# Weight pieces one step behind their inputs, two banks of their own, and the inverse one step behind the shrinkage

## The chip, the cores and the metric

The kernel runs on one core of one Trainium2 chip. The metric is the device time of one execution in microseconds (us). The kernel before took 2717.28 us in the median of three runs (2714.53 to 2717.35).

## The reference, cut to what matters

```python
def _attn_ref(x, w_r, w_i, b_r, b_i):          # x: 8 x 3008 x 256
    X = np.fft.rfft(x, axis=1)
    Yr = Xr @ w_r - Xi @ w_i + b_r             # Xr, Xi: real and imaginary part of X
    Yi = Xr @ w_i + Xi @ w_r + b_i
    Yr = np.sign(Yr) * np.maximum(np.abs(Yr) - 0.01, 0.0)      # Yi in the same way
    return np.fft.irfft(Yr + 1j * Yi, n=3008, axis=1).astype(np.float32)

def _moe_ref(x, w_in, w_out):                  # x: 24064 x 256, w_in: 256 x 2048
    h = x @ w_in
    return ((h * np.cos(h)) @ w_out).astype(np.float32)
```

The result is `_moe_ref(_attn_ref(x))`. The two weights of the second part come as 64-bit floats.

## The kernel before

A sequence of 3008 = 64 x 47 points is transformed in two stages per batch. Stage A multiplies by the 47-point transform; stage B does the 64-point transform, the products with the weights, the shrinkage and the inverse of the 64 points, and writes to a scratch tensor in DRAM (`scr`). Stage C (L583 to L625) reads the scratch back (tile `bt`), does the last 47-point transform into a bank `pc` and splits the tokens into a high and a low part (`xTh`, `xTl`). The second part, `moe_step` (L657) and `second` (L628), multiplies tokens by `win` into a bank `ph` (L664 to L666), computes h cos(h) by two activations and a multiplication (L671 to L676), and multiplies by `wo` into two banks `po`. While one batch is in the second part, the stages of the next ones are mixed in between; a planner sets the order there.

Ahead of that lies a prologue, written by hand for batch 0 (`stage_b0`, L456 to L575) under `manual_schedule`, where each engine does its instructions in the written order. Its main loop has twelve steps m. A step has

- on TensorE (PE): product p1 (L499), the forward transform pb for step m + 2 (L487), two products p2 (L511), transposes pq for step m + 3 (L474), the inverse pi (L535), and in some steps one chunk `pa` of stage A for batch 1 (L307);
- on VectorE (DVE): two additions k1 (L503, L504), the sum Xf (L492), four operations on z (L519, L522) and the clamp cl of the shrinkage (L526); the subtraction z - cl (L527) is on GpSimd (POOL), in the last step on DVE;
- on ScalarE (ACT): the scaling of k1 (L505) and the copies out of the banks: X (L491), at (L477), bo (L537), ao (L309). SyncE (SP) issues the writes of bo and ao.

Between these stand the weight pieces. There are sixteen, each 128 x 512 values of 64 bits (`raw`) that `split_f64` (L174) turns into a high and a low part: Abs on ACT (L179), a clamp on POOL (L182) or DVE (L189), two word operations on DVE that build the value `wa` in a PSUM bank (L190, L192), on ACT the cast to the high part (L194) and the scaled low words `wl` (L195), two more operations on DVE (L199, L147), two on POOL (L202, L203). Six pieces are mixed into the loop, one in two steps, two follow at its end (the tail, split in the block that begins at L686), and the last eight come in the second part, through a single buffer `raw` each time. `split_f64` is a generator; each `yield` is a place where the written order goes on with something else. In the loop a piece's clamp is written directly behind its Abs, the cast directly behind the word operations.

PSUM has eight banks: three with tag f, three with h, and o0, o1. In the prologue `fps` (L234) hands out all eight in turn, to pieces as to products.

## Time and profile before

| | |
|---|---|
| median of three runs | 2717.28 us |
| profiled execution | 2712.17 us, span of its instructions 2710.4 us |
| PE busy | 2674.2 us, 99% of the span |
| DVE, ACT, POOL busy | 1773.5, 1788.3, 1014.4 us (65%, 66%, 37%) |
| granted TensorE clock over the span | 0.994 |
| chain that ended last | PE 96%, DVE 2%, ACT 1%, DMA 1% |

PE is busy almost always. The page's slices of 67.8 us show 8 and 7 tenths in the first two slices and 9 in all others, and a granted clock of 9 and 8 tenths in the first two. So the stages that matter for a change in the prologue are read by themselves, in windows and timelines of the first 150 us. In a timeline a row gives the start, the duration, the engine, the source line, what is written from what, the shape, how many instructions were merged into the row, and in brackets how long the engine was idle before and who released it. The pitch of PE instructions is read from differences of starts, since the durations of matmuls overlap.

### The profile page before, as it was taken

The numbers are of one execution on the slowest core, as the hardware profiler recorded it, in microseconds if no ns is written. First come the engines' busy times: TensorE is split into PE (matmuls) and PEld (weight loads), VectorE is DVE, ScalarE is ACT, GpSimd is POOL, SyncE is SP. The second block draws the span as 40 slices with busy tenths as digits, with TensorE's granted clock in tenths as the row PEclk, the third lists the DMA queues.
The fourth block names the chain that finished last, engine by engine and source line by source line (L and its number), as shares of the span: only waits on it lengthen the run. The fifth ranks groups of instructions, "written<-read, shape, count | busy, mean of one in ns | idle before, by whom it ended". The sixth has DMA issues, their size and how long they took to land.

```text
span 2710.4 us, 37830 instructions
## 1 busy us (share of the span) xinstructions
PE 2674.2 (99%) x13466; PEld 2276.6 (84%) x13466; DVE 1773.5 (65%) x3023; ACT 1788.3 (66%) x3392; POOL 1014.4 (37%) x875
## 2 busy tenths in 40 slices
PE   8799999999999999999999999999999999999999
PEld 6478888888888888888888888888888888888888
DVE  4676776666657666666666666666666666756665
ACT  3477666766666666666666666666676666666666
POOL 4575342444424443244432444234342333322222
PEclk9899999999999999999999999999999999999999
DMA  6432121222112221122211221112121111010000
GB/s 179 142 102 82 59 71 57 67 72 76 45 55 69 77 69 54 48 67 71 69 51 54 67 74 63 62 43 77 61 74 55 33 47 58 24 45 30 11 16 15
DMA packets 110253, 168.97 MB, mean 62 GB/s; under 512 B 11344, under 2 KB 60080, under 8 KB 110064
## 3 DMA queue, kind: packets, MB, share of 16 engines
q1 hardware_dynamic: 103216, 144.55, 17.1%
q0 software_dynamic: 6640, 21.81, 2.6%
q8 instruction: 106, 1.74, 0.3%
q14 instruction: 83, 0.68, 0.1%
q10 hardware_dynamic: 208, 0.20, 0.0%
HBM read 94.68 MB, written 71.83 MB: 61 GB/s over the span
## 4 chain that ended last, share of the span: by engine, by line
PE 96%; DVE 2%; ACT 1%; DMA 1%; POOL 0%; issue 0%; ACTq 0%; DVEq 0%; POOLq 0%
PE ph L664 13%; PE po L638 13%; PE ph L665 13%; PE po L639 13%; PE ph L666 13%; PE po L642 13%; PE pc L608 4%; PE pb L372 3%; PE p L398 2%; PE p L397 2%; PE p L396 2%; PE pi L436 2%; PE pa L340 1%; PE pa L342 1%; PE pa L341 1%; PE p L496 1%
## 5 line engine op out<-in xcount | busy, mean ns | idle before, releaser
L144 POOL TENSOR_TENSOR gl<-u,gh 128x512 fp32r<-128x512 f32 (+1 forms) x396 | 503.7, 1272 | 1104.8 <-ACT gh L676 933.1
L672 DVE SCALAR_TENSOR_TENSOR u<-ph,u 128x512 f32<-128x512 f32 (+1 forms) x768 | 520.4, 678 | 359.0 <-ACT u L671 353.6
L675 DVE TENSOR_TENSOR u<-ph,u 128x512 f32<-128x512 f32 (+1 forms) x768 | 521.3, 679 | 314.3 <-ACT u L674 299.5
L671 ACT ACTIVATE u<-ph 128x512 int32<-128x512 f32 (+1 forms) x768 | 450.5, 587 | 310.8 <-PE ph L666 303.6
L674 ACT ACTIVATE u<-u 128x512 f32<-128x512 f32 (+1 forms) x768 | 480.2, 625 | 253.2 <-DVE u L672 250.6
L664 PE MATMUL ph<-xTh,win 128*128 128x512 f32 (+1 forms) x1536 | 613.1, 399 | 3.5 <-DVE u L675 2.5
L638 PE MATMUL po<-gh,wout 128*128 128x512 f32 (+1 forms) x1536 | 601.5, 392 | 0.0
L665 PE MATMUL ph<-xTl,win 128*128 128x512 f32 (+1 forms) x1536 | 596.7, 388 | 0.0
L666 PE MATMUL ph<-xTh,win 128*128 128x512 f32 (+1 forms) x1536 | 595.3, 388 | 0.0
L639 PE MATMUL po<-gh,wout 128*128 128x512 f32 (+1 forms) x1536 | 594.6, 387 | 0.0
L676 ACT CAST gh<-u 128x512 fp32r<-128x512 f32 (+1 forms) x768 | 467.1, 608 | 156.4 <-DVE u L675 154.6
L642 PE MATMUL po<-gl,wout 128*128 128x512 f32 (+1 forms) x1536 | 475.7, 388 | 0.0
L666 PEld LDWEIGHTS ph<-xTh,win 128*128 128x128 f32 x1536 | 289.1, 188 | 56.5
L664 PEld LDWEIGHTS ph<-xTh,win 128*128 128x128 f32 x1536 | 290.2, 189 | 51.2 <-DVE u L675 3.3
L147 DVE TENSOR_TENSOR gl<-u,gh 128x512 fp32r<-128x512 f32 (+1 forms) x372 | 286.4, 770 | 68.6 <-ACT gh L676 65.1
L638 PEld LDWEIGHTS po<-gh,wout 128*128 128x128 f32 x1536 | 289.1, 188 | 49.9
L642 PEld LDWEIGHTS po<-gl,wout 128*128 128x128 f32 x1536 | 285.8, 188 | 53.6
L639 PEld LDWEIGHTS po<-gh,wout 128*128 128x128 f32 x1536 | 289.2, 188 | 49.5
L665 PEld LDWEIGHTS ph<-xTl,win 128*128 128x128 f32 x1536 | 290.1, 189 | 45.1
L422 POOL TENSOR_TENSOR z<-z,cl 128x512 f32<-128x512 f32 x84 | 110.6, 1316 | 220.2 <-DVE cl L421 220.2
L144 POOL TENSOR_TENSOR xl<-xt,xh 96x512 fp32r<-96x512 f32 x96 | 123.9, 1293 | 126.1 <-ACT xh L327 119.1
L608 PEld LDWEIGHTS pc<-last,bt 96*128 96x128 f32 x1024 | 152.2, 195 | 18.9 <-issue 4.1
(119 smaller groups left out, 2926.6 us busy)
## 6 DMA issues: line engine op xcount, KB each, us to landing
scr<-bo SPq DMA_DIRECT2D x96, 256.0 KB, 2.0
bt<-scr SPq DMA_DIRECT2D x127, 192.0 KB, 2.6
scr<-ao SPq DMA_DIRECT2D x112, 192.0 KB, 2.1
at<-scr SPq DMA_DIRECT2D x84, 256.0 KB, 2.8
xt<-in_dram SPq DMA_DIRECT2D x108, 192.0 KB, 2.6
out_dram<-ob SPq DMA_DIRECT2D x80, 256.0 KB, 2.5
fb<-in_dram POOLq DMA_DIRECT2D x48, 256.0 KB, 3.0
raw<-in_dram POOLq DMA_DIRECT2D x16, 512.0 KB, 4.1
```

Of the source, the lines that this page charges most:

```text
L144: return nc.gpsimd.tensor_tensor(out=lo, in0=x, in1=hi.bitcast(F32), op=ALU.subtract)
L638: mm(po[e][:, :n], wo[0][:, 0, f, es], gh[:, :n], start=f == first, stop=False)
L639: mm(po[e][:, :n], wo[0][:, 1, f, es], gh[:, :n], start=False, stop=False)
L642: mm(po[e][:, :n], wo[0][:, 0, f, es], gl[:, :n], start=False, stop=f == last_f)
L664: mm(h, win[:, 0, c, fs], th[:, c, :n], start=c == 0, stop=False)
L665: mm(h, win[:, 0, c, fs], tl[:, c, :n], start=False, stop=False)
L666: mm(h, win[:, 1, c, fs], th[:, c, :n], start=False, stop=c == 1)
L671: nc.scalar.activation(k[:, :n], h, AF.Identity, bias=0.25, scale=1.0 / TWO_PI)
L672: nc.vector.scalar_tensor_tensor(out=u[:, :n], in0=h, scalar=1.0 / TWO_PI, in1=k[:, :n], op0=ALU.mult, op1=ALU.subtract)
L674: nc.scalar.activation(u[:, :n], u[:, :n], AF.Sin, bias=HALF_PI, scale=TWO_PI)
L675: nc.vector.tensor_tensor(out=u[:, :n], in0=h, in1=u[:, :n], op=ALU.mult)
L676: nc.scalar.copy(gh[:, :n], u[:, :n])
```

## The change

`split_f64` has two more `yield`s, behind the Abs and behind the word operations, and `stage_b0` has a function `words(k)` that goes on with piece k by one such part. In an even step m = 2k the clamp of piece k comes first and the second pair of DVE operations of piece k - 1 behind k1; in the odd step the POOL multiplications of k - 1 come first, then the word operations of k, its cast behind the forward transform, and at the end of the step the Abs of piece k + 1. The functions `sums`, `mixed` and `shrink` become one, `pair`, in which the inverse is `idft(m - 1)` instead of `idft(m - 2)`. Pieces of the prologue take banks o0 and o1 alone; `fps` hands out f and h in turn. The two tail pieces begin inside `stage_b0`. The first bt loads all go through SP (one went through ACT), and the rest of the first stage C is written by hand too.

```diff
@@ split_f64
-    def split_f64(hi, lo, raw, ge):
+    def split_f64(hi, lo, raw, ge, bank):
...
         nc.scalar.activation(m, v.bitcast(F32), AF.Abs)
+        yield
         if ge:
...
         yield
         ve = nc.vector
-        a = fps("wa")
+        a = ps.tile([128, 512], F32, tag=bank, name="wa", bufs=1 if bank[0] == "o" else 3)
...
+        yield
         nc.scalar.copy(hi, a)
@@ fps
         if "pro" in pool:
-            if not banks:
-                banks.extend(("f", "h", "o0", "f", "h", "o1", "f", "h"))
-            tag = banks.pop(0)
-            return ps.tile([128, 512], F32, tag=tag, name=name, bufs=1 if tag[0] == "o" else 3)
+            banks.append(name)
+            return ps.tile([128, 512], F32, tag="fh"[len(banks) % 2], name=name, bufs=3)
@@ stage_b0
+        w = {}
+
+        def words(k):
+
+            if 0 <= k < EARLY_W + TAIL_W:
+                if k not in w:
+                    w[k] = piece_steps(k, k < EARLY_W, f"o{k % 2}")
+                next(w[k], None)
+
+        def pair(m, k, odd):
+            words(k - odd)
             p = fps("p1")[:, :256]
...
             nc.scalar.activation(k1[1], k1[1], AF.Copy, scale=sig[:, m:m + 1])
-            K1[m] = k1
-
-        def mixed(m):
+            words(k - 1 + odd)
+            fwd(m + 2)
+            if odd:
+                words(k)
             p, xf = fps("p2"), X.pop(m)
...
-            P[m] = p
-
-        def shrink(m):
-            p, k1 = P.pop(m), K1.pop(m)
+            turn(m + 3)
+            if m == NP - 1:
+                next(a1)
+            idft(m - 1)
             z = wk.tile([128, 2, 256], F32, tag=("z", "yh", "yl")[m % 3], name="z", bufs=2)
...
-        w = None
+        words(0)
         for m in range(NP):
-            if m % 2 == 0:
-                load(m // 2 + 2)
-            sums(m)
-            if w is not None:
-                next(w, None)
-            fwd(m + 2)
-            mixed(m)
-            turn(m + 3)
-            idft(m - 2)
-            shrink(m)
+            k, odd = divmod(m, 2)
+            if not odd:
+                load(k + 2)
+            pair(m, k, odd)
+            if odd:
+                words(k + 1)
+                if len(raws) < EARLY_W + TAIL_W:
+                    load_piece()
             if m < 2 or m in (3, 5, 7, 9):
                 next(a1)
-            if w is not None:
-                next(w, None)
-            if m % 2 == 0:
-                w = piece_steps(m // 2, True)
-                next(w)
-                if len(raws) < EARLY_W + TAIL_W:
-                    load_piece()
+        words(EARLY_W + 1)
+        words(EARLY_W - 1)
+        words(EARLY_W - 1)
         next(a1)
-        idft(NP - 2)
         next(a1)
+        for k in range(2):
+            words(EARLY_W + k)
+            words(EARLY_W + k)
         idft(NP - 1)
-        for _ in w:
-            pass
+        next(a1)
+        return w[EARLY_W], w[EARLY_W + 1]
@@ stage_c
-                (nc.scalar if (b, u) == (0, 1) else nc.sync).dma_start(
+                nc.sync.dma_start(
@@ the block that calls them
     with tc.manual_schedule():
-            stage_b0(a1)
+        tail = stage_b0(a1)
         c00 = stage_c(0, 0)
         next(c00)
-            tail = [piece_steps(EARLY_W + k, False) for k in range(TAIL_W)]
-            for _ in range(5):
-                next(a1, None)
-                for g in tail:
-                    next(g, None)
+        for g in tail:
+            next(g)
+            next(a1)
+        for g in tail:
+            next(g)
         for _ in a1:
             pass
+        for g in tail:
+            for _ in g:
+                pass
+        first.close()
-    del pool["pro"]
+        del pool["pro"]
...
```

What the built programs have in their queues is shown for three places. First ACT in the loop, one pair of steps, in the program before. Here k is the scaling of k1, Xf and at the copies of forward transform and transposes, wm, win and wl a piece's Abs, cast and low words:

```order
L179 ACTIVATE wm<-raw 128x512
L505 ACTIVATE k_566<-k_566,sig 128x256
L194 CAST win<-wa 128x512
L195 ACTIVATE wl<-raw 128x512
L491 COPY Xf<-pb 128x512
L477 COPY at_593<-pq 128x512
L537 COPY bo<-pi 128x512
L309 COPY ao<-pa 96x512
```

The same place on ACT in the changed program:

```order
L525 ACTIVATE k_569<-k_569,sig 128x256
L491 COPY Xf<-pb 128x512
L196 CAST win<-wa 128x512
L197 ACTIVATE wl<-raw 128x512
L477 COPY at_596<-pq 128x512
L506 COPY bo<-pi 128x512
L179 ACTIVATE wm<-raw 128x512
```

The X copy has moved ahead of cast and low words, and the Abs from the front of the step to its end, where it belongs to the next piece.

Second POOL in the loop, one pair of steps before (z is the subtraction of the shrinkage, wm the clamp, wq and win the multiplications):

```order
L527 TENSOR_TENSOR z<-z,cl 128x512
L182 TENSOR_SCALAR wm<-wm 128x512
L171 DMA raw<-in_dram 128x2x512
L527 TENSOR_TENSOR z<-z,cl 128x512
L465 DMA fb<-in_dram 128x512
L202 TENSOR_TENSOR wq<-wl,wq 128x512
L203 TENSOR_TENSOR win<-wr,wq 128x512
```

And POOL in the changed program, one pair:

```order
L171 DMA raw<-in_dram 128x2x512
L465 DMA fb<-in_dram 128x512
L183 TENSOR_SCALAR wm<-wm 128x512
L548 TENSOR_TENSOR z<-z,cl 128x512
L204 TENSOR_TENSOR wq<-wl,wq 128x512
L205 TENSOR_TENSOR win<-wr,wq 128x512
L548 TENSOR_TENSOR z<-z,cl 128x512
```

Clamp and multiplications now stand ahead of the z of their step instead of behind it.

Third PE and ACT behind the first ph. On PE before, from the seventh group of ph products (the one that starts at 147.67 us) to the next pc:

```order
L664 MATMUL ph<-xTh,win 128x512
L665 MATMUL ph<-xTl,win 128x512
L666 MATMUL ph<-xTh,win 128x512
L664 MATMUL ph<-xTh,win 128x512
L665 MATMUL ph<-xTl,win 128x512
L666 MATMUL ph<-xTh,win 128x512
L608 MATMUL pc<-last,bt 128x94 x8
```

On PE in the changed program, from the end of the sixth group to the seventh:

```order
L671 MATMUL ph<-xTh,win 128x512
L672 MATMUL ph<-xTl,win 128x512
L673 MATMUL ph<-xTh,win 128x512
L615 MATMUL pc<-last,bt 128x94 x8
L671 MATMUL ph<-xTh,win 128x512
```

The eight pc matmuls stood behind the eighth group and stand ahead of the seventh now. On ACT in the changed program, from the last of the first pc tiles on:

```order
L628 CAST xTh<-pc 128x2x188
L196 CAST win<-wa 128x512
L678 ACTIVATE u<-ph 128x512
L179 ACTIVATE wm<-raw 128x512
L197 ACTIVATE wl<-raw 128x512
L678 ACTIVATE u<-ph 128x512
L681 ACT_TABLE_LOAD
L681 ACTIVATE u<-u 128x512
```

And the same on ACT before, from the cast of the ninth piece on:

```order
L194 CAST win<-wa 128x512
L671 ACTIVATE u<-ph 128x512 x2
L674 ACT_TABLE_LOAD
L674 ACTIVATE u<-u 128x512
L671 ACTIVATE u<-ph 128x512
L674 ACTIVATE u<-u 128x512
L179 ACTIVATE wm<-raw 128x512
L195 ACTIVATE wl<-raw 128x512
```

The Abs and the low words of the tenth piece (wm and wl from raw) stood behind three activations of ph and the table load, and stand behind the first activation now.

## Rows read from the trace of the kernel before

**Rows 1.** Three stages: us; busy PE, PEld, DVE, ACT, POOL (x); PEclk; DMA share; GB/s

```profile
32.46:119.19 86.73, 67.36 (x301) 48.81 (x300) 54.73 (x119) 35.85 (x69) 44.34 (x38) 0.94 0.41 126
...
130.43:147.67 17.24, 13.98 (x51) 11.94 (x51) 8.79 (x19) 9.53 (x21) 7.64 (x7) 0.61 0.44 133
147.67:300.00 152.33, 152.33 (x726) 126.72 (x726) 105.13 (x168) 116.55 (x222) 92.18 (x77) 1.00 0.28 84
```

**Rows 2.** Waits from 36 to 122 us: who for whom, total us, times, longest

```profile
PE pb L487 <- ACT at L477: 11.8, 5, 3.2
```

**Rows 3.** Timeline, one pair of steps: start, us, engine, line [idle before, releaser]

```profile
41.75 0.69 DVE L190 TENSOR_SCALAR wa<-wm 128x512 uint32<-128x512 uint32 x1 [2.51 <-POOL wm L182]
...
45.37 1.16 PE L487 MATMUL pb<-fb,at 128*128 128x128 f32 x8 [2.32 <-ACT at L477]
...
47.60 1.26 POOL L527 TENSOR_TENSOR z<-z,cl 128x512 f32<-128x512 f32 x1 [5.30 <-DVE cl L526]
...
56.25 0.69 DVE L190 TENSOR_SCALAR wa<-wm 128x512 uint32<-128x512 uint32 x1 [2.49 <-POOL wm L182]
```

**Rows 4.** Timeline, from the last inverse to the first pc

```profile
119.19 1.28 PE L535 MATMUL pi<-z,inf 128*128 128x512 f32 x2 [2.89 <-ACT ao L309]
...
123.30 0.86 SPq L592 DMA_DIRECT2D bt<-scr  x2
...
130.43 5.46 PE L608 MATMUL pc<-last,bt 96*128 96x128 f32 x24 [3.29 <-DVE wr L147]
```

**Rows 5.** Timeline, first ph and the stop behind it

```profile
136.94 1.65 PE L664 MATMUL ph<-xTh,win 128*128 128x512 f32 x3 [1.05 <-ACT xTh L621]
...
139.81 0.60 POOL L171 DMA_DIRECT2D raw<-in_dram  x1 [4.73 <-issue]
...
144.35 0.60 ACT L671 ACTIVATE u<-ph 128x512 int32<-128x512 f32 x1 [1.23 <-PE ph L666]
...
144.97 1.28 ACT L674 ACT_TABLE_LOAD   x1
...
147.67 0.50 PE L664 MATMUL ph<-xTh,win 128*128 128x512 f32 x1 [2.21 <-DVE u L675]
```

**Rows 6.** Timeline, PE: the first p1, then one step without an idle moment

```profile
32.46 1.03 PE L496 MATMUL p<-wr,Xf 128*128 128x256 f32 x4
...
50.24 1.03 PE L496 MATMUL p<-wr,Xf 128*128 128x256 f32 x4
...
51.10 1.05 PE L487 MATMUL pb<-fb,at 128*128 128x128 f32 x8
...
51.99 1.03 PE L496 MATMUL p<-wi,Xf 128*128 128x256 f32 x4
...
53.72 0.60 PE L474 MATMUL pq<-ident,a 128*128 128x128 f32 x4
...
54.16 1.02 PE L535 MATMUL pi<-z,inf 128*128 128x512 f32 x2
...
55.02 1.02 PE L307 MATMUL pa<-xt,fa 96*96 96x512 f32 x2
...
55.88 1.03 PE L496 MATMUL p<-wr,Xf 128*128 128x256 f32 x4
```

**Rows 7.** Timeline, DVE: the shrinkage of one step, its first and last instruction

```profile
45.20 0.84 DVE L519 TENSOR_TENSOR z<-p,k 64x256 f32<-64x256 f32 x2
...
47.08 0.43 DVE L526 TENSOR_SCALAR cl<-z 128x512 f32<-128x512 f32 x1
```

**Rows 8.** Timeline in a later stage: POOL and DVE at the same time

```profile
897.21 1.29 POOL L144 TENSOR_TENSOR gl<-u,gh 128x512 fp32r<-128x512 f32 x1 [7.83 <-ACT gh L676]
...
897.48 1.31 DVE L421 TENSOR_SCALAR cl<-z 128x512 f32<-128x512 f32 x1
```

**Rows 9.** DMA issues of the page: KB each, median us to landing

```profile
bt<-scr SPq DMA_DIRECT2D x127, 192.0 KB, 2.6
...
raw<-in_dram POOLq DMA_DIRECT2D x16, 512.0 KB, 4.1
```

More of the change, by code (lines that the diff above doesn't have):

```diff
@@ L218, in load_piece, with piece_steps @@
             raws.append(load_f64(piece(W_ORDER[len(raws)])[2]))
-    def piece_steps(k, ge):
+    def piece_steps(k, ge, bank="f"):
         while len(raws) <= k:
             load_piece()
-        return split_f64(*piece(W_ORDER[k])[:2], raws[k], ge)
+        return split_f64(*piece(W_ORDER[k])[:2], raws[k], ge, bank)
     def moe_w():
@@ L459, in stage_b0 @@
         dst = scr2[0].rearrange("j g r k d -> (j g r) (k d)")
-        at, fb, X, V, P, K1 = {}, {}, {}, {}, {}, {}
+        at, fb, X, V = {}, {}, {}, {}
         def load(n):
@@ L497, in product, with idft @@
                    skip_group_check=True)
-        def sums(m):
+        def idft(m):
+            if m < 0:
+                return
+            p, y = fps("pi"), V.pop(m)
+            for lo, hi, v in ((0, 256, 0), (256, 512, 1)) if m == 0 else ((0, 512, 1),):
+                mm(p[:, lo:hi], inf[0][:, v], y[:, lo:hi], start=lo == 0, stop=hi == 512, skip_group_check=True)
+            bo = stage_out("bo")
+            nc.scalar.copy(bo, p)
+            nc.sync.dma_start(dst[:, 512 * m:512 * m + 512], bo)
+        w = {}
[6 more added lines that the diff above has]
+            words(k - odd)
             p = fps("p1")[:, :256]
@@ L528, in shrink @@
             V[m] = z
-        def idft(m):
-            if m < 0:
-                return
-            p, y = fps("pi"), V.pop(m)
-            for lo, hi, v in ((0, 256, 0), (256, 512, 1)) if m == 0 else ((0, 512, 1),):
-                mm(p[:, lo:hi], inf[0][:, v], y[:, lo:hi], start=lo == 0, stop=hi == 512, skip_group_check=True)
-            bo = stage_out("bo")
-            nc.scalar.copy(bo, p)
-            nc.sync.dma_start(dst[:, 512 * m:512 * m + 512], bo)
         next(a1)
@@ L685, in tile_body @@
     mw = moe_w()
-    with ExitStack() as first:
-        pool["pro"] = first.enter_context(tc.tile_pool(name="pro", bufs=1))
-        idle = wk.tile([128, 512], F32R, tag="cl", name="idle", bufs=1)
-        nc.vector.memset(idle.bitcast(F32), 0.0)
-        def warm(n):
-            p = ps.tile([128, 512], F32, tag="o0", name="pz", bufs=1)
-            for _ in range(n):
-                mm(p, idle[:, :128], idle, start=True, stop=True)
-        warm(WARM)
-        stage_a0()
-        load_fourier_w()
-        inf[0] = pool["pro"].tile([128, 2, 128], F32, name="inf", bufs=1)
-        load_constants()
-        sum_fourier_w()
-        for _ in range(3):
-            load_piece()
-        with tc.issue_after(mark["x0"].ins):
-            load_split_constants()
-        split_fourier_w()
-        a1 = stage_a1()
-        with tc.manual_schedule():
-            stage_b0(a1)
-            c00 = stage_c(0, 0)
-            next(c00)
-            tail = [piece_steps(EARLY_W + k, False) for k in range(TAIL_W)]
-            for _ in range(5):
-                next(a1, None)
-                for g in tail:
-                    next(g, None)
-            for _ in a1:
-                pass
@@ L719, in tile_body, with warm @@
-    del pool["pro"]
-    pool["mo"] = ctx.enter_context(tc.tile_pool(name="mo", bufs=2, reuse_waits="tile"))
-    for _ in c00:
-        pass
+    first = ExitStack()
+    pool["pro"] = first.enter_context(tc.tile_pool(name="pro", bufs=1))
+    idle = wk.tile([128, 512], F32R, tag="cl", name="idle", bufs=1)
+    nc.vector.memset(idle.bitcast(F32), 0.0)
+    def warm(n):
+        p = ps.tile([128, 512], F32, tag="o0", name="pz", bufs=1)
+        for _ in range(n):
+            mm(p, idle[:, :128], idle, start=True, stop=True)
@@ new lines, in tile_body @@
+    warm(WARM)
+    stage_a0()
+    load_fourier_w()
+    inf[0] = pool["pro"].tile([128, 2, 128], F32, name="inf", bufs=1)
+    load_constants()
+    sum_fourier_w()
+    for _ in range(3):
+        load_piece()
+    with tc.issue_after(mark["x0"].ins):
+        load_split_constants()
+    split_fourier_w()
+    a1 = stage_a1()
+    with tc.manual_schedule():
+        tail = stage_b0(a1)
+        c00 = stage_c(0, 0)
+        next(c00)
+        for g in tail:
[3 more added lines that the diff above has]
+            next(g)
+        for _ in a1:
+            pass
+        for g in tail:
+            for _ in g:
+                pass
+        first.close()
+        del pool["pro"]
+        pool["mo"] = ctx.enter_context(tc.tile_pool(name="mo", bufs=2, reuse_waits="tile"))
+        for _ in c00:
+            pass
```

## The prediction

> **What bounds the kernel now.** I read the page first: TensorE is busy for 99% of the span, so only its idle moments and its slow clock can be won back, and the page's slices show them in the first 150 us alone. Then the windows view by stage: from the first p1 product to the last inverse PE is busy for 67.36 of 86.73 us, from the first pc to the stop behind the first ph products for 13.98 of 17.24 us at a mean granted clock of 0.61, and from there to 300 us for all of 152.33 us [rows 1]. So what the change wins in the loop of twelve steps and in the passage to the second part reaches the end of the kernel, because behind 147.67 us TensorE has no gap that could swallow it.
>
> Then the waits view of the loop: the largest wait of PE is pb on the copy of the transpose, ACT at L477, five times, 11.8 us [rows 2]. The timeline says what holds ACT: pairs of steps repeat every 14.50 us (L190 at 41.75 and 56.25 us), and a pair is one chain. DVE sits 2.51 us until POOL has clamped the piece (L182), ACT's cast L194 stands ahead of the X copy and the at copy and waits for DVE's two word operations, and PE's pb comes after that with 2.32 us idle; POOL's subtraction of z has itself waited 5.30 us for DVE [rows 3]. Nobody is full: everybody waits for an operation whose input was started just before.
>
> At the end of the loop 11.24 us pass between the last inverse (119.19) and the first pc (130.43), the last 3.29 of them for a DVE operation of a tail piece whose wa sat in a bank that pc needs, although the first bt load had been issued at 123.30 [rows 4]. From pc to the first ph 6.51 us pass, and from there to the seventh L664 (147.67) another 10.73 us, at whose end PE stands still for 2.21 us until DVE's multiplication frees a bank of ph [rows 5].
>
> **The change part by part.** No arithmetic is added or removed: the same operations of pieces, products and inverses are written in another order, the eight prologue pieces take banks o0 and o1, the rest rotates over six banks instead of eight.
>
> *The loop.* Every operation of a piece is now issued one step after its input, so cast L196 finds its wa done, and the X copy goes ahead of it; the at copy has no piece's chain before it. What remains is PE's own work. One step without an idle moment gives the pitches by differences of starts: p1 0.86, pb 0.89, the two p2 products 1.73, transposes 0.44, inverse 0.86, a chunk of the other batch 0.86 us [rows 6]. Between the first p1 and the last inverse the new order has 12 p1, 12 p2, 10 pb, 9 groups of transposes, 11 inverses and 9 chunks: 10.3 + 20.8 + 8.9 + 4.0 + 9.5 + 7.7 = 61.2 us. DVE is busy for 54.73 us in the old loop and does the same work [rows 1], so it fits beside.
>
> Moving the inverse from two steps behind to one takes slack away. Between the end of p2 and the inverse of the same step PE now has transposes, inverse, p1, pb, p2, transposes: 0.44 + 0.86 + 0.86 + 0.89 + 1.73 + 0.44 = 5.22 us. The shrinkage needs 1.88 us on DVE to the start of cl (45.20 to 47.08), 0.52 from there to POOL's start (47.60) and 1.26 on POOL [rows 3, 7]: 3.66 us. 1.56 us are left per step. Only the last step has less: behind the last p2 stand one inverse and three chunks, 3.44 us, so the last inverse waits at least 0.2 us.
>
> POOL works more during DVE's cl than before, when it always waited for cl. The price of such a meeting stands in a later stage: a cl that starts 0.27 us after a POOL operation takes 1.31 us, and it takes 0.43 in the loop of before [rows 7, 8]. That is 0.9 us each. The Trainium skill, "SBUF — State Buffer", section "Who interferes with whom", states such a lock: DVE and GpSimd share one port pair, and whoever comes second is blocked for the other's whole instruction; the two rows agree, since cl ended 0.29 us after the POOL operation did. By that rule all twelve cl and the last subtraction on DVE could be hit; by the loop's own rows none was.
>
> In the order of POOL the clamp or the two multiplications now end before the z of their step, so I expect one hit, at the last z, where the last multiplications run. I take 0.2 + 0.9 and another 1.4 us for waits in single steps that no row prices: 2.5 us, between 0 (PE never waits) and 12 (the first rival). The last inverse then starts at 32.46 + 61.2 + 2.5 = 96.2 us instead of 119.19: a gain of 23.0 us.
>
> *From the last inverse to pc.* No piece lies in a bank of pc any more, so pc waits for its data alone. Inverse to bt issue took 4.11 us (119.19 to 123.30) [rows 4], and bt lands after 2.6 us in the median [rows 9]: 6.7 us. ACT now has two Abs and two chunk copies ahead of the last bo copy, each with a buffer to wait for, so I take 8.0, between 6.7 and the old 11.24: a gain of 3.2 us.
>
> *From pc to ph* all sixteen pc matmuls come first (twelve before), 6.51 us in the old run; I take 6.0, between 4.5 at full clock and 6.5: 0.5 us.
>
> *The stop behind the first ph.* ACT's order changes for the worse: the Abs of the next piece, which needs the next raw transfer, now stands behind one activation of ph, before the second activation and the table load. That transfer is issued on POOL when the words of the piece before have been read, 2.87 us after the first ph in the old run [rows 5]; the new order does this earlier, I take 1.0 us after. Landing takes 4.1 us [rows 9], three ACT instructions of at most 0.60 us follow, and from table load to the restart of PE 2.70 us passed [rows 5]: 1.0 + 4.1 + 1.8 + 2.7 = 9.6, and I take 10.0 us against 10.73, between 8 and 14: a gain of 0.7. PE stands still longer, but eight pc matmuls that came after the restart now come before it, 8 x 0.22 (a quarter of pb's pitch) = 1.8 us of work inside the stop.
>
> *The clock.* The old run lost 0.39 of 17.24 us, 6.7 us of full-speed work, to the granted clock around the passage [rows 1], partly while waiting anyway. PE goes idle there again, before pc and behind the first ph, so part of the slow stretch may reach past the restart: a loss of 3 us, between 0 and 6.7.
>
> Sum: 23.0 + 3.2 + 0.5 + 0.7 + 1.8 - 3.0 = 26.2 us. The sum was made on the profiled execution, 2712.17 us (span 2710.4 and 1.8 around it), which becomes 2686 us. The median of the runs shown is 2717.28, 5.1 above it; the forecast in those terms is 2717.3 - 26.2 = 2691 us.
>
> **Rivals.**
>
> *Half of the loop's gaps come back.* If cl meets POOL in most steps, DVE has 54.73 + 12 x 0.9 = 65.5 us of work against PE's 61.2, and 0.9 of each step's 1.56 us of slack is gone. With that the loop would last some 9.5 us longer than I take it (4.3 from DVE's load, some 0.45 in each of eleven steps from late z), so 2700 us. For it speaks the 1.31 us cl [rows 8]; against it that POOL's work has a step of lead and ends before cl.
>
> *No change that can be measured.* The remaining eight pieces pass through one raw buffer; if their pace set the second part, an earlier start would only wait for them, and the time would be 2717 less 0 to 5 us, about 2714. Against it: PE was busy for all of the 152.33 us in which they arrived [rows 1].
>
> *Slower.* The Abs waiting for a raw transfer now stands ahead of activations of ph. If not only the first of the seven raw transfers of the second part stops PE but all of them do, each costs what the first costs. Between the first ph and its stop PE had 10.73 - 2.21 = 8.52 us of work at a mean clock of 0.61 [rows 1, 5], 5.2 us at full clock; four pc go out of it (0.9) and eight come in (1.8), 6.1 us, so that 3.9 of the 10.0 us are stop. Seven times that is 27 us; with the gain of the loop alone it makes 2717 - 23 + 27 + 5 (six such stops would also let the clock fall; I put a quarter of 3.9 us on each) = 2726 us. It decides from some 3.4 us per piece on. Against it: in the old run raw transfers came just as late for ACT, and PE did not stop [rows 1]; the later ones have three steps of finished activations in hand.
>
> **How the numbers follow.** Forecast 0.77, half of the loop 0.13, no change 0.06, slower 0.04. The forecast's own range by its bounds is 2684 to 2698 us (clock at nothing and no waits in the loop; or the passage and the stop at their upper ends). The range for 8 in 10 reaches over the first rival: 2685 to 2705. Within 0.2% (5.4 us, about what a measurement here can tell from no change) lies the second rival and a bit of the others: 0.07; faster 0.89; slower 0.04.
>
> **What would show it.** Right: in the new profile PE's gaps before pb are gone, pairs repeat every 10 to 11 us instead of 14.50, the last inverse starts at 95 to 98 us, the first pc waits for a transfer and not for DVE, the first ph comes at 109 to 112 us, and PE stands still behind it for 4 to 5 us until a DVE multiplication that hangs on raw. Wrong: PE waiting at the inverse for POOL's z in most steps, cl of 1 us and more in the loop, a last inverse behind 105 us, or idle PE behind 150 us.

## The result and the profile after

The changed kernel took 2685.09 us in the median of four runs (2682.84 to 2687.74), beside 2717.32 us of the kernel before (four runs, 2714.53 to 2718.47): a ratio of 0.9883, 95% interval 0.9866 to 0.9900. The forecast was 2691 us with a range of 2685 to 2705, so the time lies just inside the range's lower edge. The profiled execution took 2687.74 us, with a span of 2686.0 us against 2710.4.

The windows by stage, as in [rows 1]: loop, passage with the stop, and the time from the restart to 300 us (columns: us; busy PE, PEld, DVE, ACT, POOL; PEclk; DMA share; GB/s):

```profile
34.54:96.72 62.18, 61.33 (x303) 47.11 (x301) 53.74 (x119) 36.55 (x69) 44.41 (x38) 1.00 0.56 177
106.22:122.47 16.25, 12.20 (x67) 11.16 (x67) 8.88 (x19) 8.44 (x19) 4.88 (x5) 0.82 0.61 186
122.47:300.00 177.53, 177.28 (x830) 147.14 (x831) 125.49 (x202) 132.88 (x252) 104.02 (x87) 0.98 0.25 78
```

The loop is 62.18 us long where it was 86.73, and PE is busy in all of it but 0.85 us, with the same work as before on DVE (53.74 us against 54.73). Of the 24.55 us gained, 18.52 are idle time of PE (19.37 us before) and 6.03 are shorter busy time for the same matmuls (67.36 to 61.33 us): the mean granted clock rose from 0.94 [rows 1] to 1.00, so PE ran at 2.4 GHz throughout, where it had run at 1.2 GHz for a part of the time. That the loop began 2.08 us later than in the old trace (34.54 against 32.46) took part of the gain back; the first experiment shows that executions of one program differ by as much.

The wait of 11.8 us of pb for ACT [rows 2] is gone. These are waits of the new loop (who for whom: total us, times, longest):

```profile
POOL z L548 <- DVE cl L547: 14.8, 11, 3.6
...
ACT at L477 <- PE pq L474: 8.4, 5, 1.9
...
ACT win L196 <- DVE wa L193: 2.5, 4, 0.7
...
ACT wout L196 <- DVE wa L193: 1.7, 2, 1.1
```

ACT's at copy now waits for PE and no longer PE for it: the direction of the wait has turned, which is what a stage looks like when PE has become its bound. The cast still waits for DVE, for 0.7 us at most in the four pieces of `win` and for 1.1 at most in the two of `wout`. One pair of steps, as in [rows 3]:

```profile
50.62 1.05 PE L487 MATMUL pb<-fb,at 128*128 128x128 f32 x8
...
51.12 1.28 POOL L548 TENSOR_TENSOR z<-z,cl 128x512 f32<-128x512 f32 x1 [1.31 <-DVE cl L547]
...
51.74 0.68 DVE L191 TENSOR_SCALAR wa<-wm 128x512 uint32<-128x512 uint32 x1
...
53.19 0.58 ACT L196 CAST win<-wa 128x512 fp32r<-128x512 f32 x1 [0.62 <-DVE wa L193]
...
62.17 0.68 DVE L191 TENSOR_SCALAR wa<-wm 128x512 uint32<-128x512 uint32 x1
```

The word operation L191 starts with no wait for the clamp (2.51 us before), pb with no wait for ACT, and a pair repeats after 10.43 us (51.74 to 62.17) instead of 14.50. From the last inverse to the first pc, as in [rows 4]:

```profile
96.72 1.12 PE L504 MATMUL pi<-z,inf 128*128 128x512 f32 x2 [0.86 <-DVE z L548]
...
98.45 0.59 ACT L506 COPY bo<-pi 128x512 f32<-128x512 f32 x1
...
99.07 0.34 SPq L507 DMA_DIRECT2D scr<-bo  x1
...
103.34 1.31 SPq L599 DMA_DIRECT2D bt<-scr  x3
...
106.22 5.21 PE L615 MATMUL pc<-last,bt 96*128 96x128 f32 x24 [4.08 <-DMA bt<-scr]
```

The first pc waits for the transfer alone: ACT copies bo 1.73 us behind the start of the inverse, SP issues the write 0.62 us later, the bt issue comes 4.27 us behind that, and the load takes 2.88. And the stop behind the first ph, as in [rows 5]:

```profile
112.56 0.94 PE L671 MATMUL ph<-xTh,win 128*128 128x512 f32 x3
...
114.08 0.60 POOL L171 DMA_DIRECT2D raw<-in_dram  x1 [6.05 <-ACT xTh L628]
...
116.74 1.92 PE L615 MATMUL pc<-last,bt 96*128 96x94 f32 x16
...
118.05 0.67 ACT L179 ACTIVATE wm<-raw 128x512 f32<-128x512 f32 x1 [2.72 <-DMA raw<-in_dram]
...
119.77 1.28 ACT L681 ACT_TABLE_LOAD   x1
...
122.47 0.80 PE L671 MATMUL ph<-xTh,win 128*128 128x512 f32 x1 [3.81 <-DVE u L682]
```

ACT stands 2.72 us before the Abs of the tenth piece, the table load comes only then, and PE stands still for 3.81 us until DVE's multiplication.

### The profile page after: what moved, and what is told of

It is laid out like the page before. It is cut to its first block, busy times and chain, and to the rows that moved or that the text cites. A ratio compares the mean times of both kernels' runs of the same rounds, so it can differ in the third digit from the quotient of the medians.

```text
span 2686.0 us, 37841 instructions
## 1 busy us (share of the span) xinstructions
PE 2664.3 (99%) x13466; PEld 2272.8 (85%) x13466; DVE 1772.8 (66%) x3023; ACT 1789.5 (67%) x3392; POOL 1014.4 (38%) x875
## 4 chain that ended last, share of the span: by engine, by line
PE 97%; DMA 1%; DVE 1%; ACT 0%; issue 0%; SPq 0%; POOL 0%; ACTq 0%; DVEq 0%
PE ph L671 13%; PE po L645 13%; PE po L646 13%; PE ph L672 13%; PE po L649 13%; PE ph L673 13%; PE pc L615 4%; PE pb L372 3%; PE p L398 2%; PE p L397 2%; PE p L396 2%; PE pi L436 2%; PE p L496 1%; PE pa L340 1%; PE pa L342 1%; PE pa L341 1%
## 5 line engine op out<-in xcount | busy, mean ns | idle before, releaser
L683 ACT CAST gh<-u 128x512 fp32r<-128x512 f32 (+1 forms) x768 | 466.9, 608 | 153.6 <-DVE u L682 151.8
L615 PEld LDWEIGHTS pc<-last,bt 96*128 96x128 f32 x1024 | 151.1, 194 | 19.9 <-ACT wm L179 4.9
```

The source lines that it names most:

```text
L683: nc.scalar.copy(gh[:, :n], u[:, :n])
```

## The experiments

The theory was that the chain between the engines made the old loop long: an operation whose input was started just before holds up its engine's queue, and everything behind it. Rivals were that the banks or the inverse carry the gain, and later ones for the passage and the stop; a letter in an expectation stands for what that expectation says of it. All kernels were profiled, and one table reads them together, in us: first p1; loop (first p1 to last inverse); last inverse to pc; pc to the first ph; from there to the seventh matmul of the line of L664; from that to the 101st; and, as the sum of the five, first p1 to the 101st.

| kernel | median of the runs | first p1 | loop | to pc | to ph | to 7th | to 101st | sum |
|---|---|---|---|---|---|---|---|---|
| before | 2717.32 | 32.46 | 86.74 | 11.24 | 6.51 | 10.72 | 151.0 | 266.2 |
| changed | 2685.09 | 34.54 | 62.18 | 9.50 | 6.33 | 9.91 | 151.8 | 239.7 |
| changed, 2nd profile | 2682.75 | 31.17 | 62.18 | 8.29 | 4.76 | 10.40 | 150.9 | 236.5 |
| changed, 3rd profile | 2683.98 | 30.82 | 62.18 | 7.76 | 5.62 | 10.00 | 150.6 | 236.2 |
| e1 | 2688.18 | 34.92 | 65.10 | 8.91 | 6.07 | 9.75 | 151.5 | 241.4 |
| e2 | 2683.14 | 34.55 | 61.42 | 9.12 | 7.15 | 7.62 | 150.3 | 235.6 |
| e3 | 2711.03 | 31.40 | 86.07 | 8.63 | 10.19 | 9.86 | 151.0 | 265.8 |
| e4 | 2707.19 | 34.16 | 87.05 | 6.70 | 5.07 | 10.62 | 151.1 | 260.6 |
| e5 | 2692.69 | 34.79 | 67.81 | 11.86 | 6.80 | 8.84 | 149.5 | 244.8 |
| e6 | 2680.88 | 31.61 | 61.41 | 9.38 | 7.14 | 7.87 | 150.1 | 235.9 |
| e6, 2nd profile | 2682.78 | 34.72 | 61.41 | 9.46 | 7.15 | 7.55 | 150.2 | 235.8 |
| i1 | 2680.53 | 31.96 | 62.18 | 7.99 | 7.15 | 7.87 | 150.2 | 235.4 |
| i2 | 2684.48 | 34.67 | 62.18 | 8.48 | 5.55 | 9.55 | 150.7 | 236.5 |
| i4 | 2683.77 | 36.32 | 61.15 | 8.13 | 8.74 | 7.27 | 150.4 | 235.7 |

From the 101st matmul to the last one it is 2407.1 us in each of these profiles. So nothing that was done here reaches behind the first 300 us, and one execution differs from another by its sum and its first p1.

**The changed kernel again, twice**, as an anchor beside other kernels.

> The changed kernel itself, as the anchor for the three others of this set. Both theories: 2680 to 2688 us, with the first p1 product at 32 to 35 us, the last inverse 61 to 63 us behind it, and PE idle for 3 to 4 us behind the first ph products.

> The changed kernel once more, beside the kernel of e6 on the same chip. 2680 to 2688 us; loop 62.18 us whatever the opening takes; PE stops 3 us or more behind the first ph products or runs on a slow clock there.

Measured: 2682.75 us (2681.25 to 2684.94; ratio 0.9888, 0.9875 to 0.9902) and 2683.98 us (2680.54 to 2686.52; 0.9894, 0.9877 to 0.9910). The loop is 62.18 us in all three profiles of the program, and the first p1 comes at 34.54, 31.17 and 30.82 us. Two details of the second profile missed what was expected: its first p1 is earlier than 32 us, and PE stood still behind the first ph products for 4.29 us and not 3 to 4. In the third it was 2.48 us, at a granted clock of 0.80 from the first ph to that stop. The later start of the first profile is thus not the change's: the opening alone differs by up to 3.7 us between executions of one program, and the kernels of before (32.46, 31.40) lie within that. What remains of the spans is compared from the first p1 on, by the sum: 266.2 less 239.7, 236.5 and 236.2, a gain of 26.5, 29.7 and 30.0 us.

**e1: the old banks.** The changed kernel with the rotation over eight banks, to pieces as to products.

```diff
-        a = ps.tile([128, 512], F32, tag=bank, name="wa", bufs=1 if bank[0] == "o" else 3)
+        a = fps("wa")
```

> The changed kernel, except that pieces and products rotate through all eight banks as in the kernel before. Theory A (the gain of the loop comes from the order of the pieces' operations, banks matter only where pc waits for a piece): the loop from the first p1 to the last inverse stays at 62 to 65 us, the passage to pc grows by 0 to 3 us, the whole is 0 to 5 us slower than the changed kernel, 2685 to 2690 us. Theory B (the banks carry much of the gain): the loop is 70 us or longer, the whole above 2697 us.

Measured: 2688.18 us (2683.17 to 2689.84; 0.9908, 0.9894 to 0.9923). The loop is 2.92 us longer (65.10, just over the 62 to 65 of theory A and far from theory B's 70); p2 waits twice for a bank that a piece still reads, 2.3 us together. This is one of the two:

```profile
48.42 1.13 PE L498 MATMUL p<-wi,Xf 128*128 128x256 f32 x4 [1.15 <-DVE wr L147]
```

**e2: the old inverse.** The changed kernel with the inverse two steps behind the shrinkage.

```diff
-            idft(m - 1)
+            idft(m - 2)
...
         next(a1)
+        idft(NP - 2)
         next(a1)
```

> The changed kernel, except that the inverse stands two steps behind the shrinkage, as in the kernel before. Theory A: PE never waited for z with 1.6 us of slack, so more slack wins nothing in the loop (61 to 63 us); the last inverse stands behind one more inverse instead of a wait, so the whole is within 3 us of the changed kernel, 2682 to 2688 us. Theory C (the inverse's place carries part of the gain): the loop grows by 5 us or more, the whole is above 2690 us.

Measured: 2683.14 us (2677.98 to 2683.95; 0.9889, 0.9874 to 0.9904). The loop is 0.76 us shorter without this part of the change, since the last inverse no longer waits for z.

**e3: the banks alone**, in the kernel before: pieces of the prologue in o0 and o1, the rest over f and h.

```diff
-            if not banks:
-                banks.extend(("f", "h", "o0", "f", "h", "o1", "f", "h"))
-            tag = banks.pop(0)
-            return ps.tile([128, 512], F32, tag=tag, name=name, bufs=1 if tag[0] == "o" else 3)
+            banks.append(name)
+            return ps.tile([128, 512], F32, tag="fh"[len(banks) % 2], name=name, bufs=3)
```

> The kernel before, with the two banks for pieces alone and six for the rest, the order of operations as before. Theory A: the loop keeps its 86.7 us, the pairs their 14.5 us; pc no longer waits for DVE's wr, which wins 3 us of the passage at most: 2712 to 2719 us. Theory B (banks): the loop shortens by 8 us or more, the whole is below 2708 us.

Measured: 2711.03 us (ten runs, 2708.84 to 2713.90), before 2712.9 (19 runs); ratio 0.9995, 0.9985 to 1.0004: no change, though the median lies 1 us below what was expected. The passage to pc is 2.6 us shorter (8.63 for 11.24), as theory A allowed, but pc to ph is 3.7 us longer, where the second group of pc waits 3.21 us for ACT's copy of a chunk (ao). The loop is 86.07 us and waits as before:

```profile
DVE wa L190 <- POOL wm L182: 15.8, 6, 3.3
...
PE pb L486 <- ACT at L476: 10.3, 5, 3.2
```

**e4: the word operations directly behind the clamp.** The changed kernel, but in the pieces of the loop DVE's two word operations are written directly behind POOL's clamp; the cast stays a step behind them.

```diff
             nc.gpsimd.tensor_scalar(out=c, in0=m, scalar1=F64_TINY, scalar2=F64_HUGE, op0=ALU.max, op1=ALU.min)
-        yield
+        if not ge:
+            yield
...
         yield
+        if ge:
+            yield
         nc.scalar.copy(hi, a)
```

> The changed kernel, except that the two word operations of a piece on DVE are written directly behind POOL's clamp again; cast and low words on ACT keep their later place. Theory A (each operation that stands directly behind its input holds up its whole engine): DVE waits for the clamp (1.92 us, itself behind two DMA issues of POOL) in each pair, k1 and z come later by that and the inverse waits for z: pairs of 12.5 to 14.5 us, loop of 73 to 84 us, the whole 2696 to 2708 us. Theory D (the place of the cast on ACT ahead of the X and at copies was the cause by itself): the loop stays below 66 us, the whole below 2690 us.

Measured: 2707.19 us (ten runs, 2706.04 to 2708.73; 0.9978, 0.9968 to 0.9988). The loop is 87.05 us, longer than expected and as long as in the kernel before, and DVE waits for the clamp in every pair; this is one of the six:

```profile
49.71 1.93 POOL L183 TENSOR_SCALAR wm<-wm 128x512 f32<-128x512 f32 x1
...
51.68 0.69 DVE L192 TENSOR_SCALAR wa<-wm 128x512 uint32<-128x512 uint32 x1 [4.45 <-POOL wm L183]
...
53.52 0.51 ACT L528 ACTIVATE k<-k,sig 128x256 f32<-128x256 f32 x1 [6.00 <-DVE k L526]
...
54.40 0.59 ACT L480 COPY at<-pq 128x512 f32<-128x512 f32 x1
...
55.04 1.62 PE L490 MATMUL pb<-fb,at 128*128 128x128 f32 x8 [2.99 <-ACT at L480]
```

The row to read is DVE's: 4.45 us of waiting for the clamp, with the two k1 additions queued behind, so ACT's scaling waits 6.00 us, X and at copies come behind it, and pb is 2.99 us late. So one operation written directly behind its input is enough to lose as much as the whole change had won in the loop.

It is not the old link put back, though. In the kernel before, the clamp stood at the end of one step and the word operations behind the k1 additions of the next; here both stand at the front of a step, ahead of k1, and the clamp behind two DMA issues of POOL. The waits of DVE for the clamp are half as long again as they were. The first line is of the kernel before, the second of e4 (36 to 122 us):

```profile
DVE wa L190 <- POOL wm L182: 16.3, 6, 3.3
...
DVE wa L192 <- POOL wm L183: 24.8, 6, 4.6
```

Nor does the sum of 24.8 us explain the 24.87 us of the loop one to one, near as the two figures are. Of what PE lost, 17.58 us are idle time and 7.29 are longer busy time, at a mean granted clock of 0.94 instead of 1.00. The windows row of the loop:

```profile
34.16:121.21 87.05, 68.62 (x304) 49.93 (x303) 55.48 (x120) 36.23 (x71) 44.47 (x38) 0.94 0.42 131
```

**e5: the cast behind the word operations again.** The changed kernel, but cast and low words are written directly behind the word operations.

```diff
-        yield
         nc.scalar.copy(hi, a)
         nc.scalar.activation(low, pair[:, :, 0], AF.Copy, scale=2.0 ** -52)
         yield
+        yield
```

> The changed kernel, but the cast and the scaled low words of a piece on ACT are written directly behind the two word operations of DVE, as in the kernel before; the word operations stay one step behind the clamp. Theory A, with POOL to DVE as its first link: the cast waits for two word operations, 1.4 us, with only the copy of the transposes behind it, and PE's slack takes most of it: loop 0 to 4 us longer than the 62 us of the changed kernel, 2683 to 2690 us in all. Rival B (the cast ahead of the copies on ACT is what held PE): waits of pb for ACT come back, 8 us or more in the loop, 2693 us or more.

Measured: 2692.69 us (five runs, 2691.61 to 2693.35; 0.9924, 0.9912 to 0.9937), 9.9 us more than the changed kernel beside it: more than the theory said, less than the rival. My expectation overlooked that in this order the cast stands ahead of the X copy as well, not of the at copy alone:

```profile
54.19 0.59 ACT L195 CAST win<-wa 128x512 fp32r<-128x512 f32 x1 [1.09 <-DVE wa L193]
...
55.84 0.42 DVE L492 TENSOR_TENSOR Xf<-pb,Xf 128x256 f32<-128x256 f32 x1 [1.69 <-ACT Xf L491]
...
58.64 1.27 POOL L548 TENSOR_TENSOR z<-z,cl 128x512 f32<-128x512 f32 x1 [2.65 <-DVE cl L547]
...
59.96 1.13 PE L504 MATMUL pi<-z,inf 128*128 128x512 f32 x2 [0.23 <-POOL z L548]
```

DVE waits 1.69 us for X with the operations on z queued behind, so POOL and then the inverse are late, and not pb as in the rival. The loop loses 5.6 us, 2.0 of them as idle time of PE and 3.6 as longer busy time at a mean granted clock of 0.97. Another 3.6 us go in the passage (11.86 against 8.29): the cast of a tail piece stood ahead of the last bo copy, which came at 109.01 us, 6.40 behind its inverse.

**e6: the order of the pieces alone.** The edits of e1 and e2 together: old banks, old inverse.

> The changed kernel with the bank rotation of before and the inverse two steps behind, as before: what is left of the change is that every operation of a piece is written one step behind its input, and with it the new order of pieces, bt loads and tail. Theory A (this order carries the gain, banks and inverse carry at most a few us): 2682 to 2692 us, a loop of 62 to 66 us. Rival (banks and order are needed together, since wa holds a bank that the loop's products want): a loop over 70 us and over 2695 us.

> The kernel of e6 (order of the pieces alone, banks and inverse as before) beside the changed kernel on the same chip. If banks and inverse carry nothing and ACT's order behind the first ph is worth what i1 showed, 1 to 4 us faster than the changed kernel, 2678 to 2684 us, with a loop of 61.4 us and a stop under 1 us behind the first ph. If the first measurement of e6 was a favourable draw, within 1 us of the changed kernel.

Measured: 2680.88 us (2678.98 to 2682.69; 0.9875, 0.9858 to 0.9891), and in a second set 2682.78 (2680.79 to 2684.02; 0.9885, 0.9871 to 0.9900) beside 2683.98 of the changed kernel. The loop is 61.41 us in both profiles, and PE is busy in all of it but 0.08 us:

```profile
34.72:96.13 61.41, 61.33 (x303) 47.16 (x302) 53.84 (x119) 36.07 (x68) 44.45 (x38) 1.00 0.56 176
```

So the order carries the whole gain of the loop; banks and inverse add nothing to it. The first set came out under the 2682 us that had been expected at the least. The waits for a bank that e1 showed do not come here: they belong to the old rotation with the new inverse. Whether e6 beats the changed kernel by some 1 us the intervals don't tell.

What e6 keeps is still a bundle. In the loop it holds the places of the word operations (e4), of the cast and the X copy (e5), of the Abs, and of POOL's clamp and multiplications, which stand ahead of z now. The last two were not tried alone, nor was any one of these moved by itself in the kernel before.

**i1: the Abs behind the Sin.** The changed kernel; the Abs of a piece of the second part may only come behind the first Sin.

```diff
-        nc.scalar.activation(m, v.bitcast(F32), AF.Abs)
+        with tc.issue_after(mark["sin"].ins) if "sin" in mark else ExitStack():
+            nc.scalar.activation(m, v.bitcast(F32), AF.Abs)
...
-        nc.scalar.activation(u[:, :n], u[:, :n], AF.Sin, bias=HALF_PI, scale=TWO_PI)
+        sin = nc.scalar.activation(u[:, :n], u[:, :n], AF.Sin, bias=HALF_PI, scale=TWO_PI)
+        mark.setdefault("sin", sin)
```

> The changed kernel, with one edit: the Abs of the pieces of the second part may only be issued behind the first Sin activation, so that ACT does two activations of ph, the table load and the Sin before it waits for the next raw transfer. Theory A (the stop of 3.81 us behind the first ph is ACT standing behind the Abs that waits for raw): PE stops for 0.5 us or less there, first ph to seventh L671-type group falls from 9.9 to about 7.6 us, and less slow clock follows; 2 to 5 us faster than the changed kernel. Rival C (PE is held by the banks of ph and the slow clock in any case): the stop stays over 2 us, or what is won comes back as a longer slow stretch; within 1 us of the changed kernel.

Measured: 2680.53 us (2678.04 to 2682.21; 0.9879, 0.9865 to 0.9892), 2.2 us under the changed kernel beside it, with overlapping ranges. The stop is gone:

```profile
114.44 1.28 ACT L682 ACT_TABLE_LOAD   x1
...
115.74 0.63 ACT L682 ACTIVATE u<-u 128x512 f32<-128x512 f32 x1
...
116.28 0.65 ACT L180 ACTIVATE wm<-raw 128x512 f32<-128x512 f32 x1
...
117.15 0.50 PE L672 MATMUL ph<-xTh,win 128*128 128x512 f32 x1 [0.45 <-DVE u L684]
```

The Abs comes behind table load and Sin and finds raw landed; PE waits 0.45 us instead of 2.48 to 4.29 in the three profiles of the changed kernel. So the stop was ACT standing before raw. e2, e6 and e6's second profile have the same ACT order of their own accord, and 7.55 to 7.87 us there. From the first ph to the 101st matmul these four profiles take 157.7 to 158.1 us, the three of the changed kernel 160.6 to 161.7: 2.5 to 4.0 us less. In the whole sum less of it is left: i1's 235.4 is 0.8 and 1.1 us under the later two profiles of the changed kernel. From pc to ph i1 needed 7.15 us, all of them busy at half the clock; this is its windows row:

```profile
102.13:109.28 7.15, 7.15 (x33) 6.90 (x33) 3.91 (x10) 3.03 (x10) 3.26 (x3) 0.50 0.85 245
```

In the second profile of the changed kernel the same stretch ran at full clock and took 4.76 us:

```profile
101.64:106.40 4.76, 3.88 (x32) 3.71 (x33) 3.50 (x10) 2.38 (x8) 2.95 (x3) 1.00 0.94 285
```

This slow stretch (1.2 GHz) lies ahead of the stop, where the two kernels have the same order on PE, ACT, DVE and POOL, so that the stop's going cannot have caused it; it only hides a part of what i1 won. PE had been idle for 2.57 us before pc in i1 and for 2.87 in the second profile of the changed kernel, so the length of that idle time doesn't tell the two apart. Why the clock fell in the one and not in the other is not shown.

**i2: the last bo first.** The changed kernel; copy and write of the last bo stand ahead of those of two chunks (put off as `store`) and of the Abs of the eighth piece.

```diff
-        words(EARLY_W + 1)
         words(EARLY_W - 1)
...
+        idft(NP - 1)
+        for store in late:
+            store()
+        words(EARLY_W + 1)
         for k in range(2):
```

> The changed kernel, with the end of the first part in another order: the copy and the write of the last bo stand ahead of the copies and writes of the two chunks before it and of the Abs of the eighth piece. Theory A (from last inverse to the first pc, PE waits for that write and for the load behind it): the last bo is issued within 1.6 us of the last inverse instead of 2.35, its write takes 2 to 3 us instead of 4.2 since no chunk is ahead of it, the stretch from last inverse to pc falls from 9.5 to 7 to 8 us, and the kernel is 1 to 2.5 us faster than the changed one. Rival: the write takes its 4 us whatever stands ahead, because other transfers fill the DMA engines; within 0.8 us of the changed kernel.

Measured: 2684.48 us (2682.49 to 2684.70; 0.9892, 0.9877 to 0.9907): no gain. ACT did copy bo earlier, 1.21 us behind the start of the inverse (96.85) instead of 1.73, but the write took its time:

```profile
98.06 0.59 ACT L515 COPY bo<-pi 128x512 f32<-128x512 f32 x1 [1.57 <-PE pi L513]
...
102.52 1.31 SPq L610 DMA_DIRECT2D bt<-scr  x3
```

4.46 us pass from the copy's start to the bt issue. By the same measure it is 4.89, 3.41 and 3.40 us in the three profiles of the changed kernel, in the same order of queues (4.27, 2.76 and 2.74 from the issue of bo). So the write differs between executions by more than its place is worth. That nothing is won is what the rival said; its reason, other transfers in the DMA engines, is not shown.

**i4: two chunks later.** i1, and two chunks of the other batch's stage A taken out of steps 7 and 9 and done behind the last inverse, their inputs loaded ahead into tiles of their own. Two of these tiles take one of the three tags of z, which rotates over the other two here. The core of the edit:

```diff
+            elif c == 6:
+                load2(10)
+                yield
+                load(6)
+                load(7)
+                yield
+                load(8)
+                load(9)
+                load2(12)
+                yield
```

> The kernel of i1 (Abs of the later pieces behind the first Sin), with two chunks of stage A for the other batch taken out of steps 7 and 9 of the loop and done behind the last inverse, where PE stood idle for 2.6 to 4.1 us before the first pc; the inputs of the late chunks are loaded ahead into tiles of their own. Theory A (PE alone sets the loop, and the passage is set by the last bo's way through DRAM): the loop falls from 62.18 by 2 x 0.86 to about 60.5 us, the idle time before pc shrinks by as much, the stretch from last inverse to pc stays at 8 to 9.5 us: 1 to 2 us faster than the changed kernel with i1's edit, 2677 to 2681 us. Rival: two more chunk writes and the loads that now come together lengthen the last bo's write and the bt loads, the passage grows by 1.7 us or more, and nothing is won or some is lost (2681 to 2685 us).

Measured: 2683.77 us (2681.34 to 2685.50; 0.9885, 0.9870 to 0.9900): nothing won, as the rival had it. The loop fell by 1.03 us where 1.72 had been expected: PE's busy time fell by 1.45, and without a chunk in the step the inverse waits for z (0.4 us of POOL beside the 0.9 of the last step). From the last inverse to pc nothing grew (8.13 us), unlike in the rival; what was saved went in the stretch from pc to ph (8.74 us), where the second pc waited 2.52 us for ACT, and ACT up to 1.81 us with a chunk's copy for an earlier chunk's write.

## Why the prediction was right, and where it was off

*The loop* was predicted by its mechanism: with every operation a step behind its input PE's own work remains, 61.2 us by pitches, and PE was busy for 61.33. e6 shows that the order alone does it, e3 that the banks alone do not. Of the chain, e4 shows what a wait for POOL's clamp at the head of DVE's step costs, at a harsher place than in the kernel before, and e5 what the cast ahead of the X copy costs; how the old 24.6 us divide among the links is not shown. Not every operation got a step of lead: word operations and cast stand in the same step, and the cast, which was to find wa done, waits for it up to 1.1 us. It costs PE nothing there, since the X copy goes ahead of it. The mis-sized term is the waits: 2.5 us taken, 0.85 measured. Of them 1.4 had been put in "that no row prices", and none came. That the last inverse came at 96.72 us, where 96.2 had been forecast, is in part luck: the loop was 1.5 us shorter than taken and began 2.08 us later.

*The last inverse* waited as expected, 0.86 us where 0.2 + 0.9 stood, but for another reason, so that figure is right by luck. The meeting of cl with POOL did not happen: all twelve cl of the loop took 0.43 us.

```profile
L547 DVE TENSOR_SCALAR cl<-z x12: 426/427/428, 40.1 to 95.5; 128x512 f32<-128x512 f32 x12
```

(Minimum, median and maximum in ns, first and last start.) What delayed z is DVE's own order: p2 ended about when the chunk began at 92.27 us, but two word operations of the sixth piece stood ahead of z:

```profile
92.24 0.68 DVE L191 TENSOR_SCALAR wa<-wm 128x512 uint32<-128x512 uint32 x1
92.27 1.02 PE L307 MATMUL pa<-xt,fa 96*96 96x512 f32 x2
...
92.96 0.70 DVE L193 SCALAR_TENSOR_TENSOR wa<-raw,wa 128x512 uint32<-128x512 uint32 x1
...
93.56 0.85 DVE L540 TENSOR_TENSOR z<-p,k 64x256 f32<-64x256 f32 x2
```

That is read from the rows, no run moved these two. The 0.2 us had a slip in them as well: they count 1.26 us on POOL for the last subtraction, which is on DVE and takes 0.69. From z's first operation to the inverse it took 3.16 us (93.56 to 96.72), less than the 3.44 us of PE's work. The slack of 1.56 us in the other steps held: no inverse before the last one waited, until i4 took chunks out. Where a run did let a cl start while POOL worked, in e5, it was held as the two rows of the later stage had shown [rows 8]:

```profile
61.22 1.93 POOL L183 TENSOR_SCALAR wm<-wm 128x512 f32<-128x512 f32 x1
...
62.73 0.70 DVE L547 TENSOR_SCALAR cl<-z 128x512 f32<-128x512 f32 x1
```

cl ended at 63.43, 0.28 us behind POOL's clamp. The rule of the Trainium skill, "SBUF — State Buffer", section "Who interferes with whom", agrees with this row: of GpSimd and a DVE instruction in a mode that uses the port pair they share, whichever comes second is blocked for the other's whole instruction. The changed order just keeps the two apart.

*From the last inverse to pc* 8.0 us were predicted and 9.50, 8.29 and 7.76 measured, with pc waiting for the transfer and not for DVE, as forecast. In i2 an earlier bo copy, for whose delay the prediction had added time, won nothing; what differs among the three profiles is mostly the write (4.27, 2.76 and 2.74 us to the bt issue).

*From pc to ph* 6.0 predicted, 6.33, 4.76 and 5.62 measured; the lower bound, 4.5 at full clock, for which no row stands, was 4.76 in the profile that ran so. *To the seventh group* 10.0 predicted, 9.91, 10.40 and 10.00 measured, by the steps named: raw issued 1.52 us behind the first ph (1.0 taken), the Abs 3.97 us behind that (4.1), the eight pc ahead of the restart. Two of the signs named missed by a little: the first ph came at 112.56 us (109 to 112 stood), and the idle time behind it was 3.81, 4.29 and 2.48 us (4 to 5 stood). *What follows* (1.8 less 3.0 us, a loss of 1.2) came out as a loss of 0.8 and gains of 0.1 and 0.4: if the 1.8 us are right, the slow clock cost 2.6, 1.7 and 1.4 us where 3.0 were taken.

*The sum* of 26.2 us stands against 26.5, 29.7 and 30.0 from the first p1 on, so it was 0.3, 3.5 and 3.8 us short, in the later two most of it in the waits of the loop and the clock. The larger error of the forecast was its base: I added 5.1 us because the median of three runs before lay that far above the profiled execution. Later sets put before at 2712.9 (19 runs), 2713.29 (9), 2714.62 (7) and 2713.18 (7), so most of that was the draw of three runs. In the prediction's words it is the step "the forecast in those terms is 2717.3 - 26.2": from 2713.2 the measured gains of the sum give 2683 to 2687 us, where the times are. That the result lies inside the stated range at all is luck of the set: the two later sets of the same kernel (2682.75 and 2683.98) lie just under its 2685.

*The rivals.* Half of the gaps did not come back (62.18 us). The pace of the raw buffer sets nothing, and only the first raw transfer stopped PE: the last one is issued at 177.60 us, and from 122.47 to 300 us PE was busy for 177.28 of 177.53 us. The fear that an operation standing before raw on ACT costs PE time was right for that one place, as i1 showed, and worth 2.5 to 4.0 us from the first ph on. Two sums of the rivals are off by under 1 us (4.3 + 11 x 0.45 is 9.3 where 9.5 stands, six quarters of 3.9 are 5.9 where 5 stands); no rival turns on them.

## What to carry to other kernels

Where engines run their queues in order, write an operation one step behind the one that feeds it, if that one is on another engine: what costs is not the operation that waits but all that is queued behind it (in e4 two word operations at the head of a step, and a loop 24.87 us longer with no arithmetic added). Before keeping a change of several parts, run each part alone: here one carried the gain, and the two others could have stayed as they were. And compare runs from an event behind the varying opening on, or with many runs of both kernels, when a microsecond or two matter.

## What the runs showed of the hardware that was not expected

- One program, three profiles, three openings: the first p1 at 34.54, 31.17 and 30.82 us, while the loop behind it is 62.18 us each time. In the first 30 us PE ran at a granted clock of 0.89 in the first of them and of 1.00 in the third, so part of that time was at 1.2 GHz in the one and all at 2.4 GHz in the other; it was also idle for longer (busy 21.83 us against 24.39). Why the one opening differs from the other was not tested. The windows row of the first profile (columns as above):

```profile
0.00:30.00 30.00, 21.83 (x139) 20.09 (x140) 6.72 (x11) 6.69 (x12) 12.43 (x24) 0.89 0.86 238
```

The same stretch in the third profile:

```profile
0.00:30.00 30.00, 24.39 (x166) 22.10 (x167) 7.21 (x12) 9.48 (x17) 12.44 (x24) 1.00 0.89 253
```

- Transfers that are under way together at the end of the loop take up to twice as long as over the whole run: between 85 and 105 us of the first profile raw landed after 8.5 us (4.2 in the median of the page), ao after 4.1 (2.1) and bo after 3.5 (2.0). In the third profile, from 82 to 102 us, it is 8.5, 2.7 and 2.8 us.

```profile
scr<-ao SPq DMA_DIRECT2D x6, 192.0 KB, 4.1
scr<-bo SPq DMA_DIRECT2D x4, 256.0 KB, 3.5
...
raw<-in_dram POOLq DMA_DIRECT2D x1, 512.0 KB, 8.5
```
